# Ordering edges, a fold on GpSimd and later variance products in a fused attention, Fourier-mixing and MLP kernel

## The chip, the cores and the metric

One core of one Trainium2 chip. The metric is device time in microseconds (us) of one launch. The engines are named as the profile names them: PE (TensorE matmul), PEld (its weight loads), DVE (VectorE), ACT (ScalarE), POOL (GpSimd) and SP (SyncE, which issues most DMAs).

## The reference

All sizes are 4 batches of 576 tokens with 512 channels, float32.

```python
def phi(x):                       # FAVOR+ features, 8 heads of 64, 128 features
    h = einsum(x, omega) - sum(x * x) / 2
    return exp(h - max(h)) / sqrt(128)
q_p, k_p = phi(q * scale), phi(k * scale)
x = (q_p @ (k_p.T @ v)) / (q_p @ sum(k_p) + 1e-6)          # attention
u = x + real(fft(fft(x, axis=tokens), axis=channels))       # Fourier mixing
un = (u - mean(u)) / sqrt(var(u) + 1e-6)
x = u + relu(un @ w_ch1) @ w_ch2                            # MLP 1, 512-2048-512
u = x + (x.transpose @ U @ V).transpose                     # token mixing, rank 32
out = u + relu(u @ moe2_w_ch1) @ moe2_w_ch2                 # MLP 2
```

## The kernel before

Every float32 product is taken as three products of rounded parts: an operand x is split into hi (a rounded copy, made on ACT) and lo = x - hi (made on DVE or POOL), and hi*hi, hi*lo, lo*hi are summed in PSUM. So each operand that PE reads costs one ACT copy and one subtraction before it.

Attention runs over 36 steps n of 128 tokens, two groups of 18. In a group, steps s = 0 to 8 are key steps (projection, exponentials, key-value products) and s = 9 to 17 are query steps. A query step projects the tokens of step n + 1 (`proj`), takes their maximum on DVE (`mx`, L268) and eight exponentials on ACT (`phi`, L279), transposes the features of step n on PE (`pt`, L311), multiplies those of n - 1 with the key-value sums (`pn`, L327), divides on DVE (`x`, L337) and transposes the quotient of n - 2 (`px`, L351) into the residual `uT`.

The Fourier transform is laid between these steps by the table `PLAN`: one list for each group of two batches, with the step and the pieces. `aF0ovvg` is a fold: batch a, part 0, odd half, and three letters that say where its work goes: the sum or difference of two `x` tiles (`eo`, L386), then the four butterfly operations through a scratch `e2` (L366 to L369), then the low part `zl` (L381). Their rounded copies `zh` go to ACT and wait in the list `zpend` until `zflush()` in the next step. `aL` is the fold of the odd 64 tokens. `aS2e` is a first-stage transform of PE (`ps`, L402 to L407), whose result is split into `abh` and `abl`. `aDr1` is a second-stage transform of PE (`pdq`, `pdp`), after which POOL adds four or eight strips to `uT` (L443).

The tokens are also five blocks of 512, 384, 512, 384 and 512 (blk 0 to 4) for the MLPs. For each block the layer norm needs a mean (a PE product `pmn` of the channel sums `s1`, `s2`, L591 to L594), the centred and split rows (`xh`, `xl`; block 0 in `ln_apply`, the others in `prep_lna` and `prep_lnb`) and the variance: squares on ACT, summed on POOL into `s3` (L626), a PE product `pvc` (L640), a root, and a broadcast product `prs` (L651). These preparations are Python generators; each `yield` hands back to the loop, and `tick()` advances the head of the list `jobs` by one. A tick stands behind every three matmuls of 128x512 or 128x384 in `l1` and `l2`, eight ticks in a unit.

The MLPs are 160 units (layer, block, 128 hidden rows): `l1` makes `ph`, ACT and DVE make `hh` and `hl`, `l2` sums into `acc`. The first seven units (`TAIL`) are laid into the last Fourier steps, n = 38 to 44. From unit 7 on the queue orders of PE, ACT, DVE and POOL are exactly the order of the program text (`manual_schedule`). Before that a planner orders each queue from modelled times and the priorities of the text, so an instruction may stand in front of one that the text has first. `tc.issue_after(ins)` adds an edge: what the block issues on the engine of `ins` stands behind `ins` in that engine's queue; other engines get no edge. Each queue runs in its order.

Weights come as raw 64-bit words, are converted (`conv_a`, `conv_b`: two ACT, three DVE, one addition on POOL or DVE) and split (`wsplit`: `wh` on ACT, `wl` on POOL or DVE).

Of the kernel before, what the change touches and what calls it, by code (L numbers as in the profile page):

```python
# [44 lines left out]
WL0 = 1  # L45
LNS = 23
LNC = 'v'
LNA = 'gvvgvgvg'
DIAG = [0]
CADD = 'vgvvvvvvvg'  # L50
THI = 'vaaavvvvvvvavaaaaaaaaaaavaaaaaavvaaa'
# [21 lines left out]
        (26, "bDr1"),  # L73
    ],
    [
        (13, "aF0evvv aF0ovvg"),
        (14, "aF1oggg"),
        (15, "aF1egvv aLgv"),
        (16, "aS0e"),
# [14 lines left out]
def tile_favor_fnet_moe(ctx: ExitStack, tc: tile.TileContext, qT, kT, v1, om, w1a, w2a, uu, vv, w1b, w2b, cs, cd, out):  # L94
# [22 lines left out]
            eng[e].tensor_copy(out=dst, in_=src)  # L117

    def split(dst_hi, dst_lo, src, lo_eng):
        nc.scalar.activation(dst_hi, src, AF.Copy)  # L120
        lo_eng.tensor_tensor(out=dst_lo, in0=src, in1=dst_hi.bitcast(F32), op=ALU.subtract)  # L121


    def conv_a(dst, raw, c0, n, p, nm):
# [79 lines left out]
    def lnt(tag, nm):  # L204
        return lnp.tile([128, NBX], F32, tag=tag, name=nm, bufs=2 if tag in ("ct", "sq") else 1)
# [7 lines left out]
    pla = cb.enter_context(tc.tile_pool(name="pla", bufs=2))  # L213

    NS = 36
    raw_, hl_, vt_, phi_, pj_, kvp_, kv_, qpT_, pn_, x_, xr_ = ({} for _ in range(11))

    def load(n):
# [54 lines left out]
    def exps(n, g):  # L273
        if n >= NS:
            return
        pss, mx = pj_[n]
        for hh in range(4):
            h = 4 * g + hh
            nc.scalar.activation(phi_[n][:, h, :], pss[g][:, hh, :], AF.Exp, bias=mx[:, h : h + 1])  # L279

    def kvmm(n):
        g0, s = n // 18, n % 18
# [79 lines left out]

    def fold(src, key, eng, zeng):
        z = plf.tile([128, 4, 128], F32, tag="z", name=f"z{key}", bufs=2)
        e2 = lnt("sa", f"e2{key}")[:, 0:256]
        eng.tensor_tensor(out=e2, in0=src[:, 0:256], in1=src[:, 256:512], op=ALU.add)  # L366
        eng.tensor_tensor(out=z[:, 2:4, :].rearrange("t a d -> t (a d)"), in0=src[:, 0:256], in1=src[:, 256:512], op=ALU.subtract)
        eng.tensor_tensor(out=z[:, 0, :], in0=e2[:, 0:128], in1=e2[:, 128:256], op=ALU.add)
        eng.tensor_tensor(out=z[:, 1, :], in0=e2[:, 0:128], in1=e2[:, 128:256], op=ALU.subtract)  # L369
        zh = plf.tile([128, 4, 128], F32R, tag=f"zh{key[1:]}", name=f"zh{key}")  # L370
        zl = plf.tile([128, 4, 128], F32R, tag=f"zl{key[1:]}", name=f"zl{key}")
        zs_[key] = (zh, zl)
        if key[1:] == "l2":
            for t, p, o in ((zh, slice(0, 64), slice(64, 128)), (zl, slice(64, 128), slice(0, 64))):
                zpend.append(lambda t=t, p=p, o=o: nc.scalar.activation(t[p], z[p], AF.Copy))
                zpend.append(lambda t=t, p=p, o=o: zeng.tensor_tensor(out=t[o], in0=z[p], in1=t[p].bitcast(F32), op=ALU.subtract))
        else:
            e = ZHE[18 * (int(key[0]) // 2) + len(zdone) % 18]
            zdone.append(0)
            zpend.append(lambda: copy(zh, z, e))  # L380
            zpend.append(lambda: zeng.tensor_tensor(out=zl, in0=z, in1=zh.bitcast(F32), op=ALU.subtract))  # L381
# [10 lines left out]
    def s_stage(b, kd, kind):  # L392
        if kind == "e":
            ab_[(b, kd)] = [plf.tile([128, 2, NEO], F32R, tag=f"ab{i}", name=f"ab{i}_{b}_{kd}", bufs=3) for i in "hl"]
        abh, abl = ab_[(b, kd)]
        c0, w, i0 = (0, NE, 0) if kind == "e" else (NE, NO, 292)
        ps = psf.tile([128, 512], F32, tag="pm", name=f"ps{b}_{kd}{kind}")
        for c in range(2):
            zh, zl = zs_[f"{b}{kind}{c}"]
            ch = cst[:, 0, c, i0 : i0 + 2 * w]  # L400
            cl = cst[:, 1, c, i0 : i0 + 2 * w]
            nc.tensor.matmul(ps[:, 0 : 2 * w], zh[:, kd, :], ch, start=(c == 0), stop=False)  # L402
            nc.tensor.matmul(ps[:, 0 : 2 * w], zh[:, kd, :], cl, start=False, stop=False)
            nc.tensor.matmul(ps[:, 0 : 2 * w], zl[:, kd, :], ch, start=False, stop=False)
        z = zs_[f"{b - b % 2}l2"][b % 2]
        nc.tensor.matmul(ps[:, 0 : 2 * w], z[:, kd, :], cst[:, 0, 2, i0 : i0 + 2 * w], start=False, stop=False)
        nc.tensor.matmul(ps[:, 0 : 2 * w], z[:, kd, :], cst[:, 1, 2, i0 : i0 + 2 * w], start=False, stop=True)  # L407
        pv = ps[:, 0 : 2 * w].rearrange("p (a s) -> p a s", a=2)
        split(abh[:, :, c0 : c0 + w], abl[:, :, c0 : c0 + w], pv, nc.vector)

    DST = {
# [50 lines left out]
    exps(0, 0)  # L462
    exps(0, 1)

    def zflush(k=9):
        for _ in range(min(k, len(zpend))):
            zpend.pop(0)()

    X = {}
    late = {}  # L470
# [98 lines left out]
    def ln_apply(blk, seng, eng):  # L569
        c0, nb = BLKS[blk]  # L570
        mean = LN.pop(blk)
        hi, lo = x_tiles("x", blk)
        for r in range(4):
            c = lnt("ct", f"n{blk}_{r}")[:, 0:nb]
            seng[r].tensor_tensor(out=c, in0=uT[:, r, c0 : c0 + nb], in1=mean, op=ALU.subtract)
            split(hi[:, r, :], lo[:, r, :], c, eng[r])
        X[(0, blk)] = hi, lo

    RS = {0}
# [5 lines left out]
    def prep_lna(blk):  # L585
        c0, nb = BLKS[blk]
        u = uT[:, :, c0 : c0 + nb]
        add = dict(op=ALU.add)
        s1 = lnt("sa", f"s1_{blk}")[:, 0:nb]
        s2 = lnt("sb", f"s2_{blk}")[:, 0:nb]  # L590
        nc.vector.tensor_tensor(out=s1, in0=u[:, 0, :], in1=u[:, 1, :], **add)  # L591
        nc.vector.tensor_tensor(out=s2, in0=u[:, 2, :], in1=u[:, 3, :], **add)
        yield
        nc.vector.tensor_tensor(out=s1, in0=s1, in1=s2, **add)  # L594
        for _ in range(5 if blk > 2 else 2):
            yield
        pmn = misc(f"pmn{blk}")[:, 0:nb]
        nc.tensor.matmul(pmn, ones, s1, start=True, stop=True)
        yield
        if blk > 2:  # L600
            LN[blk] = pmn
            return
        LN[blk] = mean = lnt("mean", f"mean{blk}")[:, 0:nb]
        nc.scalar.activation(mean, pmn, AF.Copy)
        yield

    def prep_lnb(blk):
# [7 lines left out]
        for r in range(6):  # L615
# [14 lines left out]
                nc.vector.tensor_tensor(out=lo[:, q, :], in0=cs_[q], in1=hi[:, q, :].bitcast(F32), op=ALU.subtract)  # L630
            yield
        X[(0, blk)] = hi, lo
        yield
        for _ in range(5):
            yield
        n = nb // 128
        pvc = misc(f"pvc{blk}")
# [201 lines left out]
    for g in range(2 * NG - 1):  # L839
        for q in range(2 * GRP):  # L840
            wq_at.setdefault(PER * g + (2 * q if g and q < 6 else 10 + q), []).append(lambda j=2 * GRP * (g + 1) + q: wjob(j))
        for q in range(GRP):
            for k in range(2):
                wq_at.setdefault(PER * g + 15 + q, []).append(lambda fi=GRP * (g + 1) + q, k=k: sjob(fi, k))
    jobs, wjobs = [], []
    turn = [0]

    def advance(js):
# [5 lines left out]
    def tick():  # L854
        turn[0] += 1
        advance(jobs)
        if turn[0] % 2 or len(wjobs) > 2:
            advance(wjobs)

    def step(i):  # L860
        l, blk, f = units[i]
        if f % GRP == 0 and i > TAIL:
            jobs.extend(g() for g in prep_at.get((l, f // GRP, blk), []))
        if i == TAIL:
            jobs.append(lnb2)
            l2(i)
        if i + 1 < NU:
            while units[i + 1][0:2] not in X:
                tick()
            while (NF * units[i + 1][0] + units[i + 1][2], 0) not in WS:  # L870
                advance(wjobs)
            l1(i + 1)
        while (NF * l + f, 1) not in WS:
            advance(wjobs)
        if i < NU - 2 and i != TAIL:
            l2(i)
        elif i == NU - 1:
            l2(i - 1, i)
        wjobs.extend(g() for g in wq_at.get(i, []))
# [27 lines left out]
    for n in range(NS + 10):  # L907
# [50 lines left out]
        else:  # L958
            if s == 0:
                num(n - 1)  # L960
                xdiv(n - 1)
                xtr(n - 2)
                cb.close()
                xps.append(ctx.enter_context(tc.tile_pool(name="xpa", bufs=1, side="right", reuse_waits="tile")))
                hp = ctx.enter_context(tc.tile_pool(name="hp", bufs=2, side="right", reuse_waits="tile"))
                mp = ctx.enter_context(tc.tile_pool(name="mp", bufs=1, side="right", reuse_waits="tile"))
                psm = ctx.enter_context(tc.tile_pool(name="psm", bufs=1, space=PSUM, side="right", reuse_waits="tile"))
                hps.extend([(psm, "h"), (psf, "pm")])
                wpools.append(mp)
                ln_apply(0, [eng[e] for e in LNA[0:4]], [eng[e] for e in LNA[4:8]])  # L970
                wsplit(0, 0, nc.vector)
                wsplit(1, 0, nc.vector)
            if s == 1:
                xtr(n - 2)
                l1(0)
                wsplit(0, 1)
                wsplit(1, 1)
                wsplit(2, 0)
                wsplit(2, 1)
                for j in (6, 7):  # L980
                    conv_b(*w_conv_a(j), nc.gpsimd)
                wsplit(3, 0)
                wsplit(3, 1)
                jobs.extend([prep_lna(1), prep_lnb(1)])
            zflush()
            for p in pieces:
                p()
            if 2 <= s < 2 + TAIL:
                step(s - 2)
            if s == 5:  # L990
# [8 lines left out]
    pz["m"] = psm2  # L999
    hps[1] = (psm2, "h")  # L1000

    while jobs:
        tick()
    lnb2 = prep_lnb(2)
    while (0, 2) not in X:
# [91 lines left out]
```

## Time and profile before

| | us |
|---|---|
| median of 3 runs | 1080.05 (1078.63 to 1084.92) |
| the profiled execution, its time | 1079.91 |
| its span, first to last instruction | 1078.1 |
| PE busy in the span | 1048.5 (97%) |
| DVE busy | 582.0 (54%) |
| POOL busy | 414.3 (38%) |
| ACT busy | 400.2 (37%) |

The span is 1.8 us shorter than the time of its own execution. A busy share is an average over the whole span; the stages differ. The granted clock of TensorE, averaged over the span, is 0.991 of full speed.

### The profile page before, as it was taken

To read this page: it belongs to the slowest core of one execution; us is meant where nothing else is said; L and a number is where in the kernel's file an instruction comes from. 1 tells how busy PE (TensorE), PEld (TensorE's weight loads), DVE (VectorE), ACT (ScalarE), POOL (GpSimd) and SP (SyncE) were. 2 spreads that over 40 slices of the span, in tenths; PEclk is the share of its full clock that TensorE was granted. 3 is DMA by queue.
4 is the path that set the end of the run, shared out by engine and by line. 5 is a ranking of instruction groups with operands and counts; after the bars stand their busy time and mean duration, and the time that the engine had idled before them with its cause. 6 is when DMAs were issued, how large, how long until landed. Compare 5 with 4: busy or idle time off the path is not lost.

```text
span 1078.1 us, 14786 instructions
## 1 busy us (share of the span) xinstructions
PE 1048.5 (97%) x5704; PEld 925.8 (86%) x5704; DVE 582.0 (54%) x1023; ACT 400.2 (37%) x894; POOL 414.3 (38%) x386
## 2 busy tenths in 40 slices
PE   8999998889889999999999999999999999999998
PEld 7989998679788889898889787789898989888996
DVE  6798788785488653445336656562433334332222
ACT  7877786543344231322222435331312132131110
POOL 2467755765436434634445246230410140131000
PEclk9999998989999999999999999999999999999999
DMA  7642320100012120111011101111111011100111
GB/s 241 195 143 54 105 60 1 40 1 1 1 59 84 48 87 21 40 59 49 30 40 59 40 1 40 39 40 40 40 43 56 20 46 52 59 1 1 69 40 69
DMA packets 47590, 56.87 MB, mean 53 GB/s; under 512 B 3040, under 2 KB 39264, under 8 KB 47392
## 3 DMA queue, kind: packets, MB, share of 16 engines
q1 hardware_dynamic: 47232, 53.23, 15.9%
q0 software_dynamic: 288, 2.70, 0.7%
q8 instruction: 45, 0.74, 0.3%
q14 instruction: 25, 0.20, 0.1%
HBM read 51.20 MB, written 4.72 MB: 52 GB/s over the span
## 4 chain that ended last, share of the span: by engine, by line
PE 87%; DVE 6%; POOL 4%; issue 1%; ACT 1%; DMA 0%; DVEq 0%; SPq 0%; POOLq 0%; ACTq 0%
PE ph L775 12%; PE ph L777 12%; PE ph L776 12%; PE acc L796 12%; PE acc L798 11%; PE acc L797 11%; PE kvp L290 3%; PE pn L327 2%; PE pj L263 1%; POOL uT L443 1%; PE pj L264 1%; PE pj L265 1%; PE pt L311 1%; POOL s L626 1%; PE mt L710 1%
## 5 line engine op out<-in xcount | busy, mean ns | idle before, releaser
L782 DVE SCALAR_TENSOR_TENSOR hl<-ph,hh 128x512 fp32r<-128x512 f32 (+1 forms) x160 | 101.9, 637 | 360.1 <-ACT hh L781 359.7
L781 ACT ACTIVATE hh<-ph 128x512 fp32r<-128x512 f32 (+1 forms) x160 | 88.9, 555 | 509.1 <-PE ph L777 508.7
L796 PE MATMUL acc<-hh,wh 128*128 128x512 f32 (+1 forms) x640 | 238.5, 373 | 0.0
L798 PE MATMUL acc<-hl,wh 128*128 128x512 f32 (+1 forms) x640 | 237.1, 371 | 0.5 <-DVE hl L782 0.5
L797 PE MATMUL acc<-hh,wl 128*128 128x512 f32 (+1 forms) x640 | 236.9, 370 | 0.0
L808 POOL TENSOR_TENSOR uT<-uT,t 128x512 f32<-128x512 f32 (+1 forms) x80 | 99.2, 1271 | 136.5 <-DVE t L807 136.5
L158 POOL TENSOR_TENSOR w<-mc,sc 128x512 uint32<-128x512 uint32 x48 | 62.9, 1310 | 213.6 <-DVE mc L155 206.9
L798 PEld LDWEIGHTS acc<-hl,wh 128*128 128x128 f32 x640 | 120.5, 188 | 17.5 <-DVE hl L782 1.4
L796 PEld LDWEIGHTS acc<-hh,wh 128*128 128x128 f32 x640 | 120.7, 189 | 17.1 <-issue 0.9
L797 PEld LDWEIGHTS acc<-hh,wl 128*128 128x128 f32 x640 | 120.7, 189 | 15.5
L775 PE MATMUL ph<-xh,wh 128*128 128x512 f32 (+1 forms) x320 | 122.3, 382 | 0.0
L776 PE MATMUL ph<-xl,wh 128*128 128x512 f32 (+1 forms) x320 | 119.9, 375 | 1.9 <-DVE xl L121 1.9
L777 PE MATMUL ph<-xh,wl 128*128 128x512 f32 (+1 forms) x320 | 119.7, 374 | 0.5 <-DVE wl L121 0.5
L775 PE MATMUL ph<-yh,wh 128*128 128x512 f32 (+1 forms) x320 | 118.7, 371 | 0.0
L777 PE MATMUL ph<-yh,wl 128*128 128x512 f32 (+1 forms) x320 | 118.6, 371 | 0.0
L776 PE MATMUL ph<-yl,wh 128*128 128x512 f32 (+1 forms) x320 | 118.5, 370 | 0.0
L834 POOL TENSOR_TENSOR wl<-w,wh 128x512 fp32r<-128x512 f32 x56 | 75.7, 1371 | 75.2 <-ACT wh L832 64.4
L279 ACT ACTIVATE phi<-pj,mx 128x128 f32<-128x128 f32 x288 | 82.2, 385 | 10.9 <-DVE mx L268 10.1
L776 PEld LDWEIGHTS ph<-xl,wh 128*128 128x128 f32 x320 | 60.8, 190 | 10.6 <-DVE xl L121 2.4
L775 PEld LDWEIGHTS ph<-xh,wh 128*128 128x128 f32 x320 | 60.8, 190 | 9.4 <-issue 1.4
L777 PEld LDWEIGHTS ph<-xh,wl 128*128 128x128 f32 x320 | 60.8, 190 | 9.1 <-DVE wl L121 0.8
L777 PEld LDWEIGHTS ph<-yh,wl 128*128 128x128 f32 x320 | 60.1, 188 | 8.2
(644 smaller groups left out, 1765.6 us busy)
## 6 DMA issues: line engine op xcount, KB each, us to landing
raw<-in_w1a_dram SPq DMA_DIRECT2D x16, 512.0 KB, 3.6
raw<-in_w2a_dram SPq DMA_DIRECT2D x16, 512.0 KB, 3.5
raw<-in_w1b_dram SPq DMA_DIRECT2D x16, 512.0 KB, 3.6
raw<-in_w2b_dram SPq DMA_DIRECT2D x16, 512.0 KB, 3.6
vt<-in_v_dram SPq DMA_DIRECT2D x18, 260.0 KB, 4.2
raw<-in_qT_dram SPq DMA_DIRECT2D x18, 256.0 KB, 3.2
raw<-in_kT_dram SPq DMA_DIRECT2D x17, 256.0 KB, 3.1
out_dram<-uT SPq DMA_DIRECT2D x11, 256.0 KB, 2.2
```

What stands on the lines that cost most here:

```text
L158: aeng.tensor_tensor(out=dst.bitcast(U32), in0=mu, in1=s, op=ALU.add)
L279: nc.scalar.activation(phi_[n][:, h, :], pss[g][:, hh, :], AF.Exp, bias=mx[:, h : h + 1])
L775: nc.tensor.matmul(ph, wh[:, c], xh[:, r, :], start=(r == 0), stop=False)
L776: nc.tensor.matmul(ph, wh[:, c], xl[:, r, :], start=False, stop=False)
L777: last[0] = nc.tensor.matmul(ph, wl[:, c], xh[:, r, :], start=False, stop=(r == 3)).ins
L781: nc.scalar.activation(hh, ph, AF.Relu)
L782: nc.vector.scalar_tensor_tensor(out=hl, in0=ph, scalar=0.0, in1=hh.bitcast(F32), op0=ALU.max, op1=ALU.subtract)
L796: nc.tensor.matmul(a[r], wh[:, c], hh, start=(q == 0), stop=False)
L797: nc.tensor.matmul(a[r], wl[:, c], hh, start=False, stop=False)
L798: last[0] = nc.tensor.matmul(a[r], wh[:, c], hl, start=False, stop=(q == GRP - 1)).ins
L808: nc.gpsimd.tensor_tensor(out=u, in0=u, in1=t, op=ALU.add)
L834: nc.gpsimd.tensor_tensor(out=lo, in0=src, in1=hi.bitcast(F32), op=ALU.subtract)
```

## The change

- `fold` of batch 2 (`aF0o` of the second group) goes from step 31 on DVE to step 30 on POOL, its low part included.
- `zflush` puts the ACT copies `zh` behind the last exponential that the text has issued by then (`lexp`), and flushes all of `zpend`.
- The scratch `e2` of a fold moves from tag `sa` (one buffer) to `sq` (two buffers); the scratch `s2` of `prep_lna` moves from `sb` to `sq`.
- `ln_apply` of block 0: one subtraction of the mean and two low parts move from POOL to DVE (`LNA`).
- `wsplit(1, 0)` and the splits of units 0 to 2 stand behind the last `xh` copy of `ln_apply` (`lxh`) on ACT. The conversions of weights 6 and 7 and the split of unit 3 move one step later, the conversions' DVE work behind the last `abl` (`labl`).
- `prep_lnb` ends when `xh` and `xl` are made. The variance part becomes `prep_rs` in a list of its own, `jobs2`, that every tick advances too; it pauses nine times before `pvc` where it paused six.
- For blocks 3 and 4, `prep_lna` pauses three times before the first sums, and eight times where it paused five before `pmn`.

```diff
-LNA = 'gvvgvgvg'
+LNA = 'gvvvvvvv'
@@
-        (13, "aF0evvv aF0ovvg"),
+        (12, "aF0oggg"),
+        (13, "aF0evvv"),
@@ def split
-        nc.scalar.activation(dst_hi, src, AF.Copy)
-        lo_eng.tensor_tensor(out=dst_lo, in0=src, in1=dst_hi.bitcast(F32), op=ALU.subtract)
+        hi = nc.scalar.activation(dst_hi, src, AF.Copy).ins
+        return hi, lo_eng.tensor_tensor(out=dst_lo, in0=src, in1=dst_hi.bitcast(F32), op=ALU.subtract).ins
@@ def fold
-        e2 = lnt("sa", f"e2{key}")[:, 0:256]
+        e2 = lnt("sq", f"e2{key}")[:, 0:256]
@@
-    def zflush(k=9):
-        for _ in range(min(k, len(zpend))):
-            zpend.pop(0)()
+    def zflush():
+        with tc.issue_after(lexp[0]) if n + 1 < NS else ExitStack():
+            while zpend:
+                zpend.pop(0)()
@@ def prep_lna
-        s2 = lnt("sb", f"s2_{blk}")[:, 0:nb]
+        s2 = lnt("sq", f"s2_{blk}")[:, 0:nb]
+        for _ in range(3 if blk > 2 else 0):
+            yield
...
-        for _ in range(5 if blk > 2 else 2):
+        for _ in range(8 if blk > 2 else 2):
             yield
@@ def prep_lnb
         X[(0, blk)] = hi, lo
-        yield
-        for _ in range(5):
+        jobs2.append(prep_rs(blk, s3))
+        yield
+
+    def prep_rs(blk, s3):
+        nb = BLKS[blk][1]
+        for _ in range(9):
             yield
@@ def tick
         advance(jobs)
+        advance(jobs2)
@@ def step
-            jobs.append(lnb2)
+            jobs.insert(0, lnb2)
@@ n = 36, s == 0
                 wsplit(0, 0, nc.vector)
-                wsplit(1, 0, nc.vector)
@@ n = 37, s == 1
-                wsplit(0, 1)
-                wsplit(1, 1)
-                wsplit(2, 0)
-                wsplit(2, 1)
-                for j in (6, 7):
-                    conv_b(*w_conv_a(j), nc.gpsimd)
-                wsplit(3, 0)
-                wsplit(3, 1)
+                with tc.issue_after(lxh[0]):
+                    wsplit(1, 0, nc.vector)
+                    wsplit(0, 1)
+                    wsplit(1, 1)
+                    wsplit(2, 0)
+                    wsplit(2, 1)
@@ after the pieces of the step
+            if s == 2:
+                with tc.issue_after(labl[0]):
+                    for j in (6, 7):
+                        conv_b(*w_conv_a(j), nc.gpsimd)
+                wsplit(3, 0)
+                wsplit(3, 1)
@@ before the manual part
-    while jobs:
+    while jobs or jobs2:
         tick()
```

## Rows read from the trace of the kernel before

**Rows 1.** The page, 40 slices of the span, PE's busy tenths and granted clock.
```profile
PE   8999998889889999999999999999999999999998
...
PEclk9999998989999999999999999999999999999999
```

**Rows 2.** Windows: stretch, its length, busy us of each engine, PEclk, DMA.
```profile
164.00:184.00 20.00, 17.13 (x130) 15.84 (x130) 16.60 (x38) 12.60 (x36) 13.80 (x16) 0.83 0.01 1
...
190.00:206.00 16.00, 12.79 (x69) 10.61 (x68) 13.59 (x22) 8.74 (x18) 14.14 (x14) 0.89 0.00 1
206.00:214.00 8.00, 6.17 (x36) 5.24 (x35) 3.88 (x9) 3.99 (x9) 5.43 (x7) 1.00 0.33 109
...
226.00:236.00 10.00, 7.26 (x23) 5.82 (x22) 8.53 (x18) 3.60 (x6) 6.48 (x8) 0.66 0.00 0
...
268.00:280.00 12.00, 8.97 (x39) 7.36 (x38) 5.53 (x9) 2.67 (x6) 9.01 (x9) 0.86 0.00 0
...
304.00:322.00 18.00, 15.26 (x83) 13.82 (x82) 17.73 (x26) 10.19 (x20) 7.38 (x5) 1.00 0.28 86
```

**Rows 3.** Waits of PE: for whom, total us, times, longest.
```profile
PE pvc L640 <- POOL s L626: 7.1, 3, 3.0
...
PE pt L311 <- ACT phi L279: 3.6, 3, 1.6
PE ph L776 <- DVE xl L121: 1.9, 1, 1.9
PE ps_3o L402 <- DVE abl L121: 1.8, 1, 1.8
...
PE pmn L598 <- DVE s L594: 1.4, 1, 1.4
```

**Rows 4.** Timeline of ACT: start, us, operation, [idle before and its releaser].
```profile
174.96 0.63 ACT L115 ACTIVATE zh2o<-z2o 128x512 fp32r<-128x512 f32 x1 [2.28 <-POOL z2o L369]
...
197.78 0.63 ACT L120 ACTIVATE xh<-n 128x512 fp32r<-128x512 f32 x1 [2.21 <-POOL n L575]
...
207.79 0.66 ACT L129 ACTIVATE mc<-raw 128x512 f32<-128x512 f32 x1 [1.35 <-POOL uT L443]
```

**Rows 5.** Timeline of DVE, 164 to 200 us.
```profile
164.14 0.92 DVE L386 TENSOR_TENSOR eo_0o<-x,x 128x512 f32<-128x512 f32 x1
...
166.40 1.51 DVE L367 TENSOR_TENSOR z2o<-eo_0o 128x256 f32<-128x256 f32 x1
...
169.32 0.68 DVE L268 TENSOR_REDUCE mx<-pj 128x4 f32<-128x512 f32 x1
...
171.19 0.66 DVE L381 TENSOR_TENSOR zl2e<-z2e,zh2e 128x512 fp32r<-128x512 f32 x1
...
194.82 3.48 DVE L121 TENSOR_TENSOR wl<-w,wh 128x512 fp32r<-128x512 f32 x2
198.22 1.75 DVE L121 TENSOR_TENSOR xl<-n,xh 128x512 fp32r<-128x512 f32 x1
```

**Rows 6.** Timeline of POOL.
```profile
163.95 0.56 POOL L117 COPY xr<-x 128x128 f32<-128x128 f32 x1 [4.67 <-DVE x L337]
...
167.98 1.27 POOL L386 TENSOR_TENSOR eo_1e<-x,x 128x512 f32<-128x512 f32 x1 [0.36 <-DVE z2o L367]
...
213.13 2.55 POOL L121 TENSOR_TENSOR wl<-w,wh 128x512 fp32r<-128x512 f32 x2
...
232.37 1.65 POOL L366 TENSOR_TENSOR e23o<-eo_1o 128x256 f32<-128x256 f32 x1 [3.44 <-DVE z3e L369]
...
235.51 1.29 POOL L381 TENSOR_TENSOR zl3e<-z3e,zh3e 128x512 fp32r<-128x512 f32 x1
...
271.14 3.05 POOL L626 TENSOR_TENSOR s<-s,q 128x512 f32<-128x512 f32 x2
```

**Rows 7.** Timeline of PE, three places.
```profile
224.04 0.39 PE L775 MATMUL ph<-xh,wh 128*128 128x512 f32 x1
...
236.86 0.40 PE L404 MATMUL ps_0e<-cst,zl3e 128*128 128x292 f32 x1
...
269.66 0.39 PE L775 MATMUL ph<-xh,wh 128*128 128x512 f32 x1
...
270.82 0.40 PE L777 MATMUL ph<-xh,wl 128*128 128x512 f32 x1
```

More of the change, by code (lines that the diff above doesn't have):

```diff
@@ L215, in tile_favor_fnet_moe @@
     NS = 36
+    lexp, lxh, labl = [None], [None], [None]
     raw_, hl_, vt_, phi_, pj_, kvp_, kv_, qpT_, pn_, x_, xr_ = ({} for _ in range(11))
@@ L278, in exps @@
             h = 4 * g + hh
-            nc.scalar.activation(phi_[n][:, h, :], pss[g][:, hh, :], AF.Exp, bias=mx[:, h : h + 1])
+            lexp[0] = nc.scalar.activation(phi_[n][:, h, :], pss[g][:, hh, :], AF.Exp, bias=mx[:, h : h + 1]).ins
     def kvmm(n):
@@ L408, in s_stage @@
         pv = ps[:, 0 : 2 * w].rearrange("p (a s) -> p a s", a=2)
-        split(abh[:, :, c0 : c0 + w], abl[:, :, c0 : c0 + w], pv, nc.vector)
+        labl[0] = split(abh[:, :, c0 : c0 + w], abl[:, :, c0 : c0 + w], pv, nc.vector)[1]
     DST = {
@@ L575, in ln_apply @@
             seng[r].tensor_tensor(out=c, in0=uT[:, r, c0 : c0 + nb], in1=mean, op=ALU.subtract)
-            split(hi[:, r, :], lo[:, r, :], c, eng[r])
+            lxh[0] = split(hi[:, r, :], lo[:, r, :], c, eng[r])[0]
         X[(0, blk)] = hi, lo
@@ L844, in tile_favor_fnet_moe @@
                 wq_at.setdefault(PER * g + 15 + q, []).append(lambda fi=GRP * (g + 1) + q, k=k: sjob(fi, k))
-    jobs, wjobs = [], []
+    jobs, jobs2, wjobs = [], [], []
     turn = [0]
```

## The prediction, made before the result was known

> **What bounds the kernel now.** Read the 40 slices first: PE is at nine tenths almost everywhere, and the slices that are not lie mostly between 160 and 330 us; two of those also show a lower clock [rows 1]. So PE is the bound, and the change can only return time in which PE stands idle or runs slowly. The windows put a number on each stretch [rows 2]: idle time is the length less PE's busy time, and clock loss is the length times what the clock lacks of 1.00.
>
> - 164 to 184 us: idle 20 - 17.13 = 2.87, clock 20 x 0.17 = 3.4; together 6.3.
> - 190 to 206: idle 3.21, clock 16 x 0.11 = 1.7; 4.9.
> - 206 to 214: idle 1.83, clock full; 1.8.
> - 226 to 236: idle 2.74, clock 10 x 0.34 = 3.4; 6.1.
> - 268 to 280: idle 3.03, clock 12 x 0.14 = 1.7; 4.7.
> - 304 to 322: idle 2.74, clock full; 2.7.
>
> That is 26.5 us, the most that the edits could return. The clock falls behind each larger gap, to the lower level of 1.2 GHz; the gaps between 206 and 214 and between 304 and 322 cost no clock. So a gap that is halved also returns its clock loss.
>
> The table of waits then names what each gap waited for [rows 3]: exponentials, a low part of block 0, an `abl`, the sums `s` of POOL before `pvc` three times, and the channel sums before `pmn`. Last, the timelines of the other queues show what stood in front.
>
> **164 to 184: the fold and the flush.** DVE runs `eo` and the four butterflies of `aF0o` from 164.14 to 169.32, and only then the maximum [rows 5]; the exponentials and PE's `pt` follow it, the first gap (about 1.6). The change takes five operations and this delay off DVE. POOL gets them: `eo` at 1.27 for 512 columns [rows 6] and four butterflies, which I estimate by width at half of that twice and a quarter twice, 1.9, with the low part that it had already. They can start in the step before, where POOL idles 4.67 us [rows 6]: hidden there. The second gap: ACT's queue has a `zh` copy that waits 2.28 us for POOL's `z2o`, ahead of exponentials whose maxima are done [rows 4]. The new edge puts the copy behind them. What is late next is ACT itself: 12.60 us busy in 20 [rows 2] becomes 12.60 in 13.7. I take 5.3 of 6.3 (bounds 2.1, below, and 6.3).
>
> The fold's six low and butterfly operations read two SBUF operands. So do the DVE subtractions beside them, and the trace shows a price: the same 128x512 subtraction took 0.66 us where POOL stood still and 1.75 beside POOL's [rows 5]. If the whole POOL fold (1.27 + 1.9 = 3.2) delayed DVE's chain, the stretch would give 5.3 - 3.2 = 2.1; that is the lower bound. The Trainium skill, "SBUF — State Buffer", section "Who interferes with whom", says that a DVE instruction with two SBUF inputs and a GpSimd one that reads SBUF exclude each other for a whole instruction. By that rule the fold's move is a swap of delays and the stretch gives the lower bound; the 1.75 us row agrees with it, but the row on the maximum, 0.68 us with a single PSUM input, says that what PE waits for is not touched. I keep 5.3.
>
> **190 to 206: block 0.** PE waits 1.9 us in `l1(0)` for a low part `xl` [rows 3]. That `xl` stands in DVE's queue behind two weight splits of together 3.48 us [rows 5], and the last `xh` waits 2.21 us for a subtraction on POOL [rows 4]. The change puts one of the two splits behind, and moves three POOL operations to DVE: 3 x 0.66 = 2.0 us more there, less what POOL no longer slows (3 x 1.09 between 0.66 and 1.75). PE has other transforms to run meanwhile. Of the 3.21 us idle I leave 0.8, spread over waits too small for the table's head. I take 4.1 of 4.9 (bounds 0 and 4.9). The other weight splits of units 0 to 2 come after the last `xh`; PE has the transforms of the next two steps before it needs them, so I cost them at nothing. Without that cover they cost up to 2.55 / 2 = 1.3 each [rows 6].
>
> **206 to 214: conversions.** A conversion on ACT waits 1.35 us for POOL's strips of `uT` [rows 4] with the `abh` copies behind it; PE waits 1.83 for an `abl`. Moving the conversions a step later and behind `labl` takes them out of the way: 1.8 (bounds 0 and 1.8). The split of unit 3 ends at 215.68 now and is first read at 224.04 [rows 6, 7]: 8.4 us of slack, of which the move takes about 4. No DMA moves with it but one prefetch of a raw weight, which isn't read until the manual part.
>
> **226 to 236: the variance of block 1.** Counting ticks, `pvc` moves three ticks back: nine matmuls. The spacing of full matmuls is (270.82 - 269.66) / 5 = 0.232 us [rows 7], so 2.1 us of the 2.7 us wait is filled and the clock stays. But what is late next is close behind. PE read the low part `zl3e` of the last folds at 236.86, the moment POOL had made it (235.51 + 1.29 = 236.80) [rows 6, 7]. PE comes 6.1 us earlier now; the folds come earlier only by what the second `e2` buffer frees: POOL idled 3.44 us for DVE's last read of the single one [rows 6]; I estimate that two thirds of that, 2.2, reach the end, since its inputs are made late too. Between 2.2 and 6.1, which is reached if the planner fills the hole with the next `l1`, I take about the middle, 3.9 (bounds 0 and 6.1).
>
> **268 to 280: block 2.** This lies in the manual part. `pvc` moves from tick 6 to tick 10: 12 x 0.232 = 2.8 us of 3.03 are filled, and the clock loss of 1.7 goes. POOL's two sums end at 274.2 [rows 6] as before. 4.4 (bounds 2.8 and 4.7).
>
> **304 to 322: blocks 3 and 4.** `pmn` has three more ticks (about 1.6 to 2.1 us) to cover 1.4 [rows 3]; the rows of block 4 are centred four ticks sooner while `pvc` comes one tick sooner, which covers the third `pvc` wait, 2.74 - 1.4 = 1.3. Block 3's `xl` comes two ticks later, at the last of the 24 ticks before its first use, with no tick to spare. DVE is 17.73 of 18 us busy [rows 2], so this could fail: I take 2.6 (bounds 0 and 2.7).
>
> **The sum.** 5.3 + 4.1 + 1.8 + 3.9 + 4.4 + 2.6 = 22.1. From this I take 4 us for new waits: the planner orders 0 to 236 us anew, and in the first query part the same edge puts `zh` copies later. (Four is two gaps of the sizes in [rows 3].) So 18 us off. The profiled execution took 1079.91, which is 0.14 below the median, so both give **1062 us**.
>
> **The rivals.**
>
> - *The folds and the shared ports bind* (0.20). The first stretch gives its lower bound 2.1, and PE waits 3.9 us for the last folds and loses the 3.4 us of clock again, so that 226 to 236 gives nothing: 2.1 + 4.1 + 1.8 + 0 + 4.4 + 2.6 - 4 = 11.0, 1069 us. For it: the copy at 236.86 was just in time. Against it: the second buffer, and `l1` work that could fill.
> - *The order written is not the order run* (0.12). The edges bind one engine each; the planner may put other work in front, and gaps of the old size return anywhere before the manual part. Only the manual part's 4.4 + 2.6 less 4 remain: 3 us, 1077.
> - *Slots of z* (0.05), the one that ends slower. A fold has two `z` buffers, freed by the `zh` copy. That copy now waits for a round of exponentials, so a later fold's first butterfly can wait at the head of DVE's queue, with the next maximum behind it. One such wait would cost like the `pt` gaps, 1.6 us at the longest [rows 3], and up to the 3.4 us of clock of their stretch, 5.0. There are eight flushes with exponentials left in the two query parts. From five such waits on the 18 us and 0.5% are used up: 1080 - 18 + 25 = 1087. Against it: the folds of a step are rarely more than two.
>
> **How the numbers follow.** The forecast has 0.63, its own range 1056 to 1067. Half a per cent, 5.4 us, is about what a measurement of this kernel tells from no change. Faster by more (below 1074.6): the forecast and the first rival, 0.83; within: the second, 0.12; slower: the third, 0.05. The range 1055 to 1076 holds all but the best end (all 26.5 returned is 1053) and the last two rivals.
>
> **What would show it.** In the profile after: no `pt` wait between 164 and 184 and a full clock there; `pvc` waits under 1 us together instead of 7.1; no `ph` wait for `xl`; the conversions behind `abl`; PE's total idle before 330 us down by some 11 us, and clock 0.99 rising to about 1.00. A `ps_0e` wait for `zl` would show the first rival, DVE idle before a butterfly for `zh` the third. A lower clock behind any new gap would make the forecast wrong fastest.

## The result, and the profile after it

The changed kernel takes 1094.71 us (median of six runs, 1090.19 to 1098.73), the kernel before 1081.51 beside it (six runs): ratio 1.012, interval 1.0085 to 1.0155. It is some 13 us slower, where 18 less were forecast, and outside the range. The profiled execution took 1094.42 us, with a span of 1092.7.

The page's 40 slices (PE's busy tenths, granted clock) answer to [rows 1]:

```profile
PE   8999899888998999999999999999999999999998
...
PEclk9998699989999999999999999999999999999999
```

The fifth slice, some 109 to 137 us, falls to a clock of 0.6, where the kernel before had 0.9. These are key steps of the second group of batches: PE waits there ahead of `kvp`, a key-value product. `PLAN` lays the last folds of the first group into them, at steps 19 and 20; the prediction speaks of the query parts alone. The windows of the stretches with losses (length, busy us of PE, PEld, DVE, ACT, POOL, granted clock), to be read as [rows 2]:

```profile
77.00:92.00 15.00, 13.23 (x72) 13.08 (x71) 10.77 (x27) 9.80 (x29) 8.38 (x10) 0.66 0.06 18
112.00:140.00 28.00, 23.32 (x120) 21.11 (x119) 14.09 (x19) 10.71 (x34) 11.49 (x14) 0.70 0.24 74
...
188.00:196.00 8.00, 5.55 (x49) 5.34 (x48) 6.92 (x16) 4.82 (x14) 6.13 (x8) 1.00 0.01 2
219.00:232.00 13.00, 9.74 (x33) 7.48 (x34) 6.35 (x13) 4.76 (x12) 7.66 (x10) 0.74 0.24 82
248.00:257.00 9.00, 4.76 (x21) 4.10 (x20) 5.70 (x12) 4.12 (x7) 3.87 (x5) 0.81 0.00 0
286.00:292.00 6.00, 5.71 (x28) 4.56 (x26) 3.82 (x6) 2.03 (x4) 5.92 (x7) 1.00 0.00 0
324.00:336.00 12.00, 8.85 (x44) 8.24 (x43) 11.08 (x16) 5.68 (x12) 4.08 (x3) 0.86 0.25 86
```

77 to 92 us loses 1.77 idle and 15 x 0.34 = 5.1 of clock; 112 to 140 loses 4.68 idle and 28 x 0.30 = 8.4. Together that is 20 us. The kernel before has 0.44 us idle over 75 to 92 and 0.23 over 112 to 140, both at full clock. The gap of 77 to 92 lies in the first query part, the other, as said, in key steps. PE's waits (for whom, total, times, longest) answer to [rows 3]:

```profile
PE kvp L292 <- ACT phi L281: 4.7, 1, 4.7
PE acc L807 <- DVE hl L791: 4.2, 2, 3.2
...
PE pj L265 <- ACT phi L281: 3.2, 3, 1.8
PE ph L784 <- DVE abl L122: 2.9, 1, 2.9
PE ps_0e L406 <- POOL zl3e L383: 2.6, 1, 2.6
PE px L353 <- POOL xr L118: 2.4, 1, 2.4
...
PE pvc L649 <- POOL s L631: 0.3, 1, 0.3
```

The waits that the edits were to remove are gone: `pvc` 0.3 for 7.1, `pt` 0.2 for 3.6, `pmn` no longer in the table. Others have come.

What stood in front at 115 us: DVE's timeline, then ACT's.

```profile
111.86 0.98 DVE L383 TENSOR_TENSOR zl1o<-z1o,zh1o 128x512 fp32r<-128x512 f32 x1
112.77 0.98 DVE L383 TENSOR_TENSOR zl1e<-z1e,zh1e 128x512 fp32r<-128x512 f32 x1
113.67 1.50 DVE L369 TENSOR_TENSOR z1e<-eo_1e 128x256 f32<-128x256 f32 x1
115.10 1.35 DVE L370 TENSOR_TENSOR z1e<-e21e 128x128 f32<-128x128 f32 x1
116.37 1.34 DVE L371 TENSOR_TENSOR z1e<-e21e 128x128 f32<-128x128 f32 x1
117.64 1.21 DVE L139 CUSTOM_DVE_ANT_0 w<-mc,sc 128x1024 uint16<-128x1024 uint16 x1
118.77 1.87 DVE L270 TENSOR_REDUCE mx<-pj 128x4 f32<-128x512 f32 x3
```
```profile
110.53 0.65 ACT L116 ACTIVATE zh1e<-z1e 128x512 fp32r<-128x512 f32 x1
...
119.55 1.14 ACT L281 ACTIVATE phi<-pj,mx 128x128 f32<-128x128 f32 x4 [6.83 <-DVE mx L270]
```

The two copies (`zh1o`, not shown, is the other) run behind a round of exponentials, at 110 us. Each holds a `z` buffer until it and the low part that follows have read it. The next fold's butterflies (`z1e`, 113.67 to 117.7) need that buffer, the maxima stand behind them, ACT idles 6.83 us for the maxima, and PE 4.68 for ACT.

### The profile page after: what moved, and what is told of

Same layout as the page of the kernel before. It is cut to its first block, busy times and chain, and to the rows that moved or that the text cites. A ratio compares the mean times of both kernels' runs of the same rounds, so it can differ in the third digit from the quotient of the medians.

```text
span 1092.7 us, 14778 instructions
## 1 busy us (share of the span) xinstructions
PE 1056.3 (97%) x5704; PEld 933.1 (85%) x5704; DVE 582.3 (53%) x1021; ACT 397.7 (36%) x894; POOL 410.7 (38%) x388
## 4 chain that ended last, share of the span: by engine, by line
PE 84%; DVE 8%; POOL 4%; ACT 1%; issue 1%; DMA 1%; SPq 0%; DVEq 0%; ACTq 0%; POOLq 0%
PE ph L784 11%; PE ph L786 11%; PE ph L785 11%; PE acc L807 11%; PE acc L805 11%; PE acc L806 11%; PE kvp L292 3%; PE pn L329 2%; PE pj L265 1%; PE pj L267 1%; PE pj L266 1%; POOL uT L445 1%; PE pt L313 1%; PE mt L719 1%; POOL uT L817 1%
```

## Experiments: the edge

Each kernel was timed in five rounds beside the kernel before (1080.7 to 1082.2 us). The first two undo and isolate the edge:

```diff
     def zflush():
-        with tc.issue_after(lexp[0]) if n + 1 < NS else ExitStack():
-            while zpend:
-                zpend.pop(0)()
+        while zpend:
+            zpend.pop(0)()
```

**no_edge** (the whole change but for these lines). 

> The whole change, but the flush of the z copies is issued as before, without the wait on the exponentials. Theory A (the edge is the culprit: in the first query part it puts the butterflies that wait for a z buffer ahead of the next maxima in VectorE's queue): the two large gaps at 77 and 115 us (1.8 and 4.7 us idle, with about 5.1 and 8.4 us of clock behind them) are gone, so about 1094.7 - 20 = 1074.5 us, 1071 to 1078. Rival B (the edge only shows a lack of VectorE and GpSimd time that the two e2 buffers and the folds make): gaps of that size come back at other folds, 1088 or more.

Measured: 1078.39 us, ratio 0.9985 (0.997 to 1.0). PE's longest wait for `phi` is 0.71. Theory A holds, 0.4 us above its interval, though only the smaller of the two gaps lies in the first query part. The two `pt` waits between 164 and 184 us, the second of which the edge was made for, are gone without it.

**only_edge** (before, with these lines alone). 

> The kernel before with nothing but the edge: z copies issued behind the exponentials of their step. Theory A (edge is the culprit): gaps in the first query part as in the changed kernel, so 1081.5 + 20 = 1101 us, less at most the 1.3 us gap and 3.4 us of clock at 174 to 184: 1095 to 1102. Rival B (the edge does harm only together with the fold that starts sooner, or with the second e2 buffer): 1077 to 1084.

Measured: 1098.96 us, ratio 1.0161 (1.0136 to 1.0186). The same `kvp` wait of 4.7 us is there, and of the two `pt` waits of the second query part one, of 1.4, stays, with a new wait of 2.0 for `den` behind it. The edge alone costs more than the whole change: theory A, and rival B falls.

**edge_z4** asks whether it is the buffers or the lateness of the copies as such:

```diff
-        z = plf.tile([128, 4, 128], F32, tag="z", name=f"z{key}", bufs=2)
+        z = (pla if key[0] in "01" else plf).tile([128, 4, 128], F32, tag="z", name=f"z{key}", bufs=4 if key[0] in "01" else 2)
```

> The run with the edge alone, with four z buffers in place of two in the first query part. The order on TensorE and ScalarE stays as in that run; on VectorE the three butterflies of z1e go ten instructions up, out of the stretch ahead of the maximum. Theory A (slots: the late copy keeps both z buffers, and the butterflies that wait for one stand ahead of the next maximum): the 4.67 us gap at 118 us loses their 3.7 us, and with it most of the 8 to 9 us of clock behind it: 1099 - 12 = 1087, 1083 to 1091. Rival B (what delays the maximum are the two low parts, which the edge makes late whatever the buffers): the gap stays over 2.5 us with its clock, 1095 to 1099.

Measured: 1085.79 us, ratio 1.0037 (1.0022 to 1.0053), 13 us less than with two buffers. The windows over that place, of only_edge and then of edge_z4, and the last two butterflies of `z1e` in edge_z4:

```profile
112.00:144.00 32.00, 27.33 (x121) 24.64 (x120) 14.87 (x20) 11.23 (x35) 14.14 (x15) 0.63 0.25 75
```
```profile
108.00:140.00 32.00, 31.18 (x238) 29.32 (x237) 23.68 (x37) 22.86 (x70) 21.14 (x23) 1.00 0.34 99
```
```profile
101.83 0.81 DVE L369 TENSOR_TENSOR z1e<-e21e 128x128 f32<-128x128 f32 x1
102.57 0.28 DVE L370 TENSOR_TENSOR z1e<-e21e 128x128 f32<-128x128 f32 x1
```

The low parts `zl1o` and `zl1e` are as late (109.28 and 110.19, for 110.48 and 111.39 in only_edge), and yet the gap falls to 0.82 and its clock loss is gone: it was the buffers.

What is left of the edge's cost is the smaller gap at 77 us (clock 0.91 over 72 to 92). Four buffers do not change it, 2.05 us idle for 2.06 in only_edge, so it is not a wait for a `z` buffer. DVE's queue has another order there. In the kernel before, a maximum stands ahead of the fold's `e20e` (first line); with the edge, both maxima stand behind `e20e` and the butterflies (the other two, of only_edge):

```profile
73.65 0.69 DVE L268 TENSOR_REDUCE mx<-pj 128x4 f32<-128x512 f32 x1
```
```profile
73.33 1.51 DVE L367 TENSOR_TENSOR e20e<-eo_1e 128x256 f32<-128x256 f32 x1
...
77.14 1.28 DVE L269 TENSOR_REDUCE mx<-pj 128x4 f32<-128x512 f32 x2
```

No run puts this order back alone, so for the smaller gap the cause is argued and not shown.

## Experiments: the other parts, each alone

**only_rs** (before, with the variance products in their own list, the pauses, and `s2` in `sq`):

```diff
+        for _ in range(3 if blk > 2 else 0):
+            yield
...
+        jobs2.append(prep_rs(blk, s3))
```

> The kernel before with nothing but the variance part: the variance products in a second list of jobs with nine pauses, three more pauses around the sums of blocks 3 and 4, s2 in a buffer of its own kind, lnb2 put in front. By the sum on record this part alone gives 3.9 + 4.4 + 2.6 = 10.9, 1070.6 us. Theory C (only block 2's gap is really returned, 4.4; block 1's goes to the last folds and block 4's low part hl comes late): about 1077, 1075 to 1079, with a wait for hl near 327 us.

Measured: 1079.04 us, ratio 0.9983 (0.9967 to 0.9999): neither 1070.6 nor 1077. Block 2's `pvc` wait falls from 3.0 to 0.3. Block 1's also goes, and behind it PE waits 2.7 for `zl3e`, 1.2 for `zl3o` and 0.6 for `zh3e`, with a clock of 0.57 over 240 to 248. The wait for `abl` grows from 1.8 to 3.6, and `hl` at 231 us takes 1.3. At 319 us `hl` takes 3.2, for the 2.7 of `pmn` and `pvc`. The profiled execution is the longest of the twelve (1083.02), so it shows more loss than the median has.

**only_plan** (before, with the fold a step sooner):

```diff
-        (13, "aF0evvv aF0ovvg"),
+        (12, "aF0oggg"),
+        (13, "aF0evvv"),
```

> The kernel before with nothing but the fold that starts a step sooner on GpSimd (its five operations move from VectorE). By the sum on record the stretch 164 to 184 us gives 5.3: 1076.3. Theory F (the xr copy and the subtraction n share GpSimd's queue with the folds; without the edge and with all else as before, px waits for them): the pt waits of 1.6 and 1.3 us go and a px wait of 2 to 3 us comes, 1079 to 1082.

Measured: 1077.79 us, ratio 0.9964 (0.9949 to 0.998): 3.9 us of the 5.3, a little better than theory F gave, and with its mark, a `px` wait of 1.9 for POOL's `xr`. The `pt` waits between 164 and 184 us are gone here too, with no edge.

**only_x0** (before, with block 0's part):

```diff
-LNA = 'gvvgvgvg'
+LNA = 'gvvvvvvv'
...
+                with tc.issue_after(lxh[0]):
+                    wsplit(1, 0, nc.vector)
...
+                with tc.issue_after(labl[0]):
+                    for j in (6, 7):
+                        conv_b(*w_conv_a(j), nc.gpsimd)
```

> The kernel before with nothing but block 0's part: centring on VectorE, four of the five weight splits behind the last xh, the two conversions and the split of unit 3 a step later and behind labl. By the sum on record 4.1 + 1.8 = 5.9 less, 1075.6 us. Theory D (the conversions' ScalarE half is bound by no edge and still stands ahead of the abh copies, and px waits for an xr copy): the gap of 1.8 us becomes one of about 3 with 3.4 us of clock, so the part gives nothing or loses: 1080 to 1085.

Measured: 1081.85 us, ratio 1.0011 (0.9998 to 1.0023): nothing, as by theory D. The wait of 1.9 for `xl` goes, as in the sum, and one of 2.9 for an `abl` comes. **only_x0_conv** binds ACT's half too:

```diff
-        labl[0] = split(abh[...], abl[...], pv, nc.vector)[1]
+        labl[:] = split(abh[...], abl[...], pv, nc.vector)
...
-                with tc.issue_after(labl[0]):
+                with tc.issue_after(labl[0]), tc.issue_after(labl[1]):
```

> The run of block 0's part alone (1081.9), with the two conversions behind the last abh copy on ScalarE as well. The sum on record gives 4.1 + 1.8 = 5.9 for this part: 1081.5 - 5.9 = 1075.6. Theory D (the part was right and only the edge bound the wrong engine): the gap of 2.93 us at 207 us with 2 to 3 us of clock goes, 1075 to 1078. Rival (block 0's part gives nothing even so): 1080 or more.

Measured: 1080.18 us, ratio 0.9982 (0.9971 to 0.9992), at the edge of the rival's "1080 or more". The first line is of PE's waits in only_x0, the second in only_x0_conv:

```profile
PE ph L780 <- DVE abl L121: 2.9, 1, 2.9
```
```profile
PE pvc L645 <- POOL s L627: 11.6, 3, 7.2
```

The 2.9 us are gone, and block 1's `pvc`, at 3.2 in only_x0, waits 7.2. PE came sooner to sums that were no sooner done. So D names the cause of its gap, but a gap removed here is not yet time gained.

## Experiments: repairs of the change without the edge

The windows of no_edge close the account (columns as above):

```profile
100.00:106.00 6.00, 4.85 (x40) 4.61 (x40) 5.36 (x11) 5.19 (x14) 4.27 (x7) 1.00 0.27 88
152.00:160.00 8.00, 7.20 (x59) 6.61 (x59) 7.06 (x22) 6.54 (x17) 5.49 (x7) 1.00 0.01 2
168.00:184.00 16.00, 13.56 (x104) 13.16 (x102) 11.37 (x30) 10.70 (x32) 12.53 (x16) 0.89 0.01 2
184.00:200.00 16.00, 15.00 (x102) 13.14 (x101) 14.54 (x35) 11.78 (x26) 4.12 (x7) 1.00 0.01 2
200.00:216.00 16.00, 12.45 (x62) 10.40 (x61) 8.20 (x15) 6.95 (x17) 11.70 (x13) 0.89 0.19 66
216.00:248.00 32.00, 27.38 (x133) 23.61 (x132) 24.15 (x42) 10.64 (x23) 19.92 (x26) 0.84 0.00 1
264.00:280.00 16.00, 15.71 (x86) 14.01 (x85) 11.49 (x18) 5.73 (x11) 12.84 (x14) 1.00 0.01 1
302.00:320.00 18.00, 14.81 (x84) 13.52 (x83) 17.23 (x26) 8.17 (x18) 6.23 (x5) 1.00 0.26 80
```

Idle and clock together, the prediction's stretch before in brackets: 168 to 184 loses 4.2 (6.3), to 200 1.0 (4.9), to 216 5.3 (1.8), to 248 9.7 (6.1), 264 to 280 0.3 (4.7), 302 to 320 3.2 (2.7), and 2.0 are new at 100 and 152. In all 25.7, for 26.5 before. The change without its edge gives back 10.4 us in three places and loses 9.6 in the others. The repairs go to the places of loss.

**no_edge_conv_xl** binds the conversions as in only_x0_conv, and moves two low parts of block 4 to POOL:

```diff
-                nc.vector.tensor_tensor(out=lo[:, q, :], ...)
+                (nc.gpsimd if blk == 4 and q % 2 else nc.vector).tensor_tensor(out=lo[:, q, :], ...)
```

> The change without the edge, with two edits in stretches far apart: the two conversions are put behind the last abh copy on ScalarE too (not only behind the last abl on VectorE), and two of block 4's four low parts go from VectorE to GpSimd. Theory D (an edge to a VectorE instruction leaves the conversion's ScalarE half ahead of the abh copies): the gap of 2.95 us at 208 us and about 1.4 of clock go, 4 us. Theory E (304 to 322 us is bound by VectorE, 17.7 of 18 us busy before, so the idle of pmn and pvc only came back as a wait for hl): the gap of 3.19 us falls to 1.5 or less. Together 1078.4 - 4 - 2 = 1072, 1070 to 1074. Rivals: what waits is GpSimd's strips, and TensorE waits for the next thing behind them; GpSimd's subtractions slow VectorE as much as they relieve it: 1077 to 1080.

Measured: 1072.97 us, ratio 0.9923 (0.9902 to 0.9944). The 2.95 us are gone (theory D); the next wait, `hh` at 226 us, grows from 1.7 to 6.1. `hl` falls only from 3.19 to 2.88: theory E, as put, fails. The time came out as forecast, but not by its terms: E gave almost nothing. Where the other 5 us came from, this trace does not show. The profiled execution is the longest of the six (1076.40), and over 60 to 340 us it loses 27.8 us of idle and clock together, for 27.5 in no_edge.

**no_edge_xr_sum** moves one `xr` copy and takes the old pauses:

```diff
-XR = 'gggvggggggggggaggg'
+XR = 'gggvgggggggggaaggg'
...
-        for _ in range(3 if blk > 2 else 0):
-            yield
```

> The change without the edge, with two edits in stretches far apart: one xr copy goes from GpSimd to ScalarE, and the sums of blocks 3 and 4 get back the pauses that they had before. Theory F (the fold and the subtraction n of GpSimd, now in one queue, keep this xr copy and with it px): the gap of 2.42 us at 176 us goes, with 1.7 us of clock. For 304 to 322 us, theory E (VectorE is the bound): the wait moves back to pmn (1.4) and pvc, with a sum of 2.5 to 3 us as in both kernels; rival (the pauses chosen are at fault): the wait for hl of 3.2 us goes and only pmn's 1.4 returns. 1078.4 - 4.1 = 1074.3 by F and E, 1072.5 by F and the rival, 1078 if px only waits for the next thing.

Measured: 1079.56 us, ratio 0.9981 (0.9968 to 0.9993). Theory F holds for the wait: POOL's queue in no_edge shows why it was there,

```profile
172.58 0.73 POOL L369 TENSOR_TENSOR z2o<-eo_1o 128x256 f32<-128x256 f32 x1
...
174.54 1.45 POOL L577 TENSOR_TENSOR n<-uT,mean 128x512 f32<-128x512 f32 x1
175.93 0.47 POOL L118 COPY xr<-x 128x128 f32<-128x128 f32 x1
```

and with the copy on ACT `px` does not wait. But `zl3e` waits 3.3, for 2.0 in no_edge, and the pauses make `hh` 1.5 and `hl` 2.4 of the one 3.2: no time is gained.

**no_edge_fix3**: all three. 

> The change without the edge, with all three repairs: conversions behind abh on ScalarE, the one xr copy on ScalarE, two low parts of block 4 on GpSimd. If theories D, E and F hold and add up: 1078.4 - 4 - 2 - 4 = 1068, 1065 to 1071, below both kernels. If each gap only hands its time to the next wait: 1075 to 1079.

Measured: 1072.62 us, ratio 0.9925 (0.9903 to 0.9947). The repairs do not add up: it is no faster than with two. ACT's queue ahead of the wait of 6.1 us:

```profile
217.77 0.63 ACT L116 ACTIVATE zh3e<-z3e 128x512 fp32r<-128x512 f32 x1 [3.65 <-DVE z3e L371]
...
221.81 0.52 ACT L628 ACTIVATE q<-c 128x384 f32<-128x384 f32 x1 [2.76 <-POOL s L630]
222.24 0.58 ACT L789 ACTIVATE hh<-ph 128x512 fp32r<-128x512 f32 x1
```

`hh` stands behind a square `q` that waits 2.76 us for a sum on POOL. The squares and the new `e2` buffers are both of the tag `sq`, which has two.

**fix3_e23_sa**: `e2` of the last batch back in `sa`; **fix3_e2_sa**: all of them.

```diff
-        e2 = lnt("sq", f"e2{key}")[:, 0:256]
+        e2 = lnt("sa" if key[0] == "3" else "sq", f"e2{key}")[:, 0:256]
```

> The change without the edge and with the three repairs, and the e2 buffers of the last batch's folds alone back in the single buffer that they had before. Theory G (the second e2 buffer is not free: it is one of the two that the squares of block 1 use, so with an e2 in it a square waits 2.8 us for GpSimd's sum, and the hidden activation hh behind it on ScalarE): the gap of 6.12 us at 223 us falls under 2, with 3 to 4 us of clock, 1072.6 - 7 = 1066, 1063 to 1068. Rival (the order on ScalarE, zh copies ahead of hh, and late folds make the gap): it stays, or the time only moves to the wait for zl3e: 1071 to 1075.

> As the run before, with all e2 buffers back in the single one. Theory G, extended (the diagonal dg of block 0 uses the same two buffers, and the waits for dg at 156 us, 0.8, and for abl at 102 us, 1.15, come from it too): 1.5 to 2 us less than that run, about 1064. Rival (the early folds gain from two buffers, as the sum on record has it, and the last folds come later): 1068 to 1075.

Measured: 1072.09 us, ratio 0.9923 (0.9904 to 0.9942), and 1072.7, 0.9938 (0.9914 to 0.9962). The square's wait is gone and `hh` falls to 4.1, `zl3e` to 1.4, but the clock over 224 to 232 is 0.50 and 0.58. Theory G explains 2 us of the wait and nothing of the time; the second `e2` buffer is worth nothing that shows.

**e23_zl_hold** and **e2_zl_hold** take the two ends of that stretch and the last one:

```diff
-        (22, "bF0ovvv bF1evvg bF1ovgv"),
+        (22, "bF0ovvv bF1evvv bF1ovgv"),
...
-        if turn[0] % 2 or len(wjobs) > 2:
+        if (turn[0] % 2 or len(wjobs) > 2) and not hold[0]:
             advance(wjobs)
```

(`hold` is set while block 4 is centred.)

> The change without the edge, with the conversions behind abh and the xr copy on ScalarE, the last batch's e2 in the single buffer, the low part zl3e of the last even fold on VectorE, and no weight conversions while block 4 is centred (all low parts of block 4 on VectorE again). Theory H (TensorE waits for zl3e because GpSimd has it last in its queue, behind a whole fold): the wait of 3.2 us falls under 1.2. Theory I (in 304 to 322 us it is the conversions, 1.4 us each beside GpSimd, that stand ahead of hl): the wait of 2.9 falls under 1. Together 4 us below the first run of this call, about 1062. Rivals: VectorE has no time for zl3e either; the conversions held back are late at the next weight: no gain.

> As the run before, with all e2 buffers in the single one: by theory G, extended, 1060; by its rival 1064 to 1070.

Measured: 1067.71 us, ratio 0.9887 (0.9867 to 0.9907), and 1067.85, 0.9884 (0.9863 to 0.9904). These beat both kernels, by 1.1% and 2.3%. The wait for `zl3e` is gone (theory H), and that for `hl` too, with a wait of 1.0 for `rc` in its place (theory I). Block 4's low parts are all on DVE in both, as in no_edge, so the held conversions are the difference in that stretch. In no_edge one can see what stood there:

```profile
313.06 1.38 DVE L152 TENSOR_SCALAR mc<-mc 128x512 uint32<-128x512 uint32 x1
314.36 0.55 DVE L790 SCALAR_TENSOR_TENSOR hl<-ph,hh 128x384 fp32r<-128x384 f32 x1
```

In e2_zl_hold two such `mc` operations still stand ahead of `hl`, but behind POOL's sums, and take 0.42 and 0.43 us.

The `hh` wait of 4.1 us is left. **best_zh_behind_hh** puts `zh3e` behind `hh` (first line), **best_fold_behind_hl** also the pieces of steps 39 and 40 behind the low part of unit 2 on DVE:

```diff
+        with tc.issue_after(lhh[0]) if n == 40 else ExitStack():
             while zpend:
...
+            with tc.issue_after(lhl[0]) if n == 40 else ExitStack():
...
+            if n in (39,):
+                with tc.issue_after(lhl[0]):
+                    for p in pieces:
+                        p()
```

> The best run so far (1067.85) with one zh copy, that of the last batch's first fold, behind the hidden activation hh of unit 2 on ScalarE. Theory J (this copy, which waits 5 us for its butterflies, holds hh): the gap of 4.1 us at 221 us and 4 us of clock behind it go: 1060, 1058 to 1063. Rival K (the fourth high part of block 1 also stands ahead of hh, its centred row waits for the fold's butterflies on VectorE through a shared buffer, and that is just as late): the gap stays over 3 us, 1066 to 1069.

> As the run before, and the last batch's first two folds stand on VectorE behind the low part hl of unit 2, so that the centred row of block 1 no longer waits for their butterflies. Theory K: the gap of 4.1 us at 221 us goes, the last folds come some 3 us later: 1067.9 - 8 + 4 = 1064, 1059 to 1066. Theory J alone gives the same time as the run before. Rival (the last folds are the bound: all that is gained at 221 us is lost at the wait for zl3e): 1067 to 1071.

Measured: 1068.98 us, ratio 0.9884 (0.987 to 0.9899), and 1067.91, 0.988 (0.9864 to 0.9897). The first lines of PE's waits in each (that for `omr` at the start left out):

```profile
PE acc L807 <- ACT hh L792: 4.1, 1, 4.1
...
PE acc L809 <- DVE hl L793: 2.1, 1, 2.1
```
```profile
PE ps_0e L404 <- ACT zh3e L116: 4.5, 1, 4.5
```

Theory J falls: the copy was not what held `hh`. What did is the fourth `xh`, here in best_zh_behind_hh, whose centred row `c` stands behind the fold's butterflies in DVE's queue (217.87 to 219.43 us):

```profile
220.22 0.52 ACT L628 ACTIVATE xh<-c 128x384 fp32r<-128x384 f32 x1 [5.91 <-DVE c L625]
```

Theory K is right about the wait, which goes when the fold goes, and its rival about the time: the same microseconds are lost a little later, at the fold that was put off.

## Why the prediction was wrong

**The step that failed** is the last of the sum, "From this I take 4 us for new waits", and in it "in the first query part the same edge puts `zh` copies later", which I priced by gaps of the old sizes. The edge cost 17.4 us alone (1.0161), and some 14.6 in the change (1.012 less 0.9985). Some 13 us of it are one wait for a `z` buffer, which four buffers take away (edge_z4). That mechanism was in the text as the third rival, at 0.05. I set such a wait at 5.0 with its clock and asked for five; one did it, with 13.1 us, beside the gap at 77 us, 6.9 with its clock, which four buffers leave as it is.

The count was wrong twice. The edge acts at ten flushes, and I counted the eight of "the two query parts": the other two are in the key steps 20 and 21, and there the large wait came, not "in the first query part". And "the folds of a step are rarely more than two" is no argument against it: two folds in a step hold both buffers, and steps 19 and 20, next to each other, have two each. The sign that I named was wrong as well: DVE is not idle before the butterflies. The planner put the late low parts and the butterflies in one row, so DVE is busy for 7 us with no maximum among them.

**164 to 184, 5.3:** 3.9 came by itself. The `pt` waits went as worked out, and without the edge. One row was read loosely: a maximum stands at 164.98, between `eo` and the butterflies, and only the next one waits until 169.32. The butterflies that I estimated at 1.9 us on POOL took 2.8 (0.73, 0.73, 0.91 and 0.46 in only_plan). What I left out is what else POOL's queue holds there: an `xr` copy on which `px` waits. Every operation that moved to POOL was costed, and not who stands behind it.

**190 to 214, 4.1 and 1.8:** in sum nothing came (only_x0), and 2 with ACT's half bound too (0.9982). The wait for `xl` went as worked out, but the one for `abl` grew from 1.8 to 2.9. I wrote of the edges that they bind one engine each, in a rival, and did not ask it of `labl`: the conversions start with two ACT instructions, and these stayed ahead of the `abh` copies. In the changed kernel they waited twice for POOL's strips, which now stood behind weight splits:

```profile
217.79 0.67 ACT L130 ACTIVATE mc<-raw 128x512 f32<-128x512 f32 x1 [1.54 <-POOL uT L445]
...
222.08 0.66 ACT L130 ACTIVATE mc<-raw 128x512 f32<-128x512 f32 x1 [2.77 <-POOL uT L445]
```

**226 to 236, 3.9:** nothing. The first rival is right for this stretch, and only here: the wait went to the last folds, as "what is late next is close behind" feared. Worse, this stretch takes back what block 0's part gains (only_x0_conv), so the terms of block 0, the conversions and block 1 were summed though they end ahead of the same late work.

**268 to 280, 4.4:** right: 4.7 became 0.3, in the changed kernel too (286 to 292).

**304 to 322, 2.6:** nothing; 3.2 for 2.7. "DVE is 17.73 of 18 us busy" was the right row, and "with no tick to spare" the right doubt. What stood in front of `hl` were weight conversions, and holding them back gave what moving two low parts to POOL did not.

**The clock**, 10.2 of the 26.5 us, was priced by the gaps: "a gap that is halved also returns its clock loss". The runs do not bear that out. The wait for `hl` took 2.88 us in no_edge_conv_xl, and the granted clock of the 10 us behind it was 0.83; it took 2.86 in no_edge_fix3, and the clock was 1.00. The wait for `xr` took 2.45 us in the changed kernel with a clock of 1.00 (188 to 204 us) and 2.42 in no_edge with 0.89 (172 to 188). So from one profile such a term is known to some 2 us.

**Left open:** why 1.8 us idle at 77 us cost 5.1 of clock in the changed kernel while 2.45 at 191 cost none; whether it is the order on DVE that makes the gap at 77 us; and what order of block 1 and the last folds would be free of waits.

## What to carry to other kernels

An edge that makes a copy later also makes the buffer that it reads free later: before adding one, list every place where it acts, in all parts of the kernel, and find there who writes into that buffer next, and what stands behind that writer in its queue. An edge binds the engine of the instruction that it names; a helper that runs on two engines needs two. Gaps in a row that end before the same late work don't add up: price them as one stretch, from the queue that ends it.

## Unexpected in the hardware

The three butterflies of `z1e` that took 1.50, 1.35 and 1.34 us took 0.42, 0.28 and 0.28 in the kernel before (from 100.69 us), where POOL stood idle for 2.22 us around them. POOL's timeline of the changed kernel over the same time:

```profile
113.28 1.61 POOL L509 TENSOR_TENSOR s<-uT 128x512 f32<-128x512 f32 x1
114.97 1.33 POOL L510 TENSOR_TENSOR s<-s,s 128x512 f32<-128x512 f32 x1
116.26 1.31 POOL L248 TENSOR_TENSOR tlo<-raw,thi 128x512 fp32r<-128x512 f32 x1
```

These end at 114.89, 116.30 and 117.57; the butterflies at 115.17, 116.45 and 117.71, each 0.14 to 0.28 us later. So the price of a short DVE operation here was that of the POOL operation beside it, whatever its width. The Trainium skill says so in "SBUF — State Buffer", section "Who interferes with whom": a DVE instruction with two SBUF inputs and a GpSimd one that reads SBUF exclude each other for a whole instruction. The trace agrees. By these rows, an estimate, this is some 3 of the 4.68 us gap (1.08 + 1.07 + 1.06 more than before).
